# Top-32 attention and a mixture of experts on one core: the query tile's fill one step earlier, a full slot chosen in nine operations, logits laid out in the order of their sum

## The chip, the core and the metric

The kernel runs on one core of a Trainium2 chip. A core has TensorE (PE, matrix products; PEld is its weight load), VectorE (DVE), ScalarE (ACT), GpSimd (POOL) and SyncE (SP), which issues most transfers. GpSimd can issue transfers too, and here it issues the indirect ones, whose rows go where a list of indices says. The metric is the device time of one execution in microseconds (us); a lower one is better.

## What is computed

The reference, cut to what matters:

```
scores = (q @ k.T) / sqrt(64)                      # batch 8, heads 8, 576 x 576
kth    = 32nd largest of each row
attn   = exp(scores - max) where scores >= kth, else 0;  divided by its sum
x      = (attn @ v), heads side by side            # 4608 tokens x 512
logits = x @ w_gate + modality_bias[modality_id]   # 8 experts
e      = argmax(logits);  gate = softmax(logits)[e]
out    = gate * (relu(x @ w1[e]) @ w2[e])          # 512 -> 1024 -> 512
```

## The kernel before

**Attention.** The 64 heads are taken in 32 pairs. A pair has nine tiles of 128 query rows: four for each head and one (role 8) that holds the last 64 rows of both. The main loop runs over steps `i`, one tile each; `p, j = divmod(i, 9)` are the pair and its step. A tile passes through the engines over several steps: TensorE makes the scores two steps ahead (`qk`), ScalarE copies them to `Ssb` (`sevac`), VectorE finds candidates with eight-way maxima (`subs`, `chain`: L375 to L388), ScalarE counts by a sign (`sign`, L407, tile `K`), GpSimd multiplies scores and signs (`pool_y`, L413, tile `y`), VectorE takes the maximum over `y` (`find`, L417) and so the 32nd value (`pick`, L424 to L426), ScalarE takes exponentials and VectorE masks and sums them (`keep`, L437); TensorE transposes and multiplies with V. `KB=2` tiles `K` and `YB=3` tiles `y` exist, so a late `y` holds up the sign two tiles on.

**GpSimd's order in a step** is the order of the code: `gate` (L460, one element, it waits for VectorE's mask of the tile before), `pool_y`, at most one indirect transfer (`posted`, `sends` or `puts`, each followed by a memset of `spare`, L516), `below` (L400, a scalar for the sign), every third step `small` (L394), and in step 5 of a pair `fill`. An engine runs its queue in order, so what stands behind a waiting instruction waits too.

**The query tile.** The role 8 tile of the next pair needs its two halves of queries as a block-diagonal matrix `qbd`. `fill` (L325) copies them from `st` in two instructions of 64 partitions each; TensorE uses the result in step 7 (`qk` of the tile two steps on, L363). In the program the second of the two waits for the completion of the indirect transfers that GpSimd issued since the fill before.

**Tokens and experts.** After each batch (four pairs) the rows are normalized, the logits formed (`logit_rows`, L544 to L564), the expert chosen (`route`), and the rows sent to lists by expert in memory: five indirect transfers, one a step (L590, `xs`). When a list holds enough rows, a slot of 256 is chosen (`sched`), its rows and weights are loaded, and TensorE works on it in the gaps (`expert`, L755 to L787), with a budget that grows by a fixed amount a step and by 0.1 for each small operation of VectorE; the 128 result rows of each half go out by an indirect transfer (L792, `puts`). `whole` says that a slot is sure to be full. The remaining slots are worked on behind the attention (from about 1030 us), with `slot` and `choose`.

**What else the change touches.** `base` and `roff` (128x8) hold where each expert's list ends and how far it has been taken; `ie` and `rev` are iotas over the experts; `dot(x, y)` multiplies with the one-hot `oh` and leaves the sum in an accumulator. `lt` holds the logits' parts (two heads `h` of four pairs `a`), over which one VectorE instruction sums.

Of the kernel before, what the change touches and what calls it, by code (L numbers as in the profile page):

```python
# [9 lines left out]
FT = mybir.dt.float32  # L10
# [62 lines left out]
def kernel(  # L73
# [120 lines left out]
    base = const.tile([128, E], FT, name="base")  # L194
    roff = const.tile([128, E], FT, name="roff")
    tokb = const.tile([128, 5], FT, name="tokb")
# [213 lines left out]
    def pool_y(i):  # L410
        t = T[i]
        t["y"] = wk.tile([128, S], FT, name="y", bufs=YB)
        G.tensor_tensor(t["y"], t["S"], t["K"], op=OP.mult)  # L413
# [134 lines left out]
    def logit_rows(u, L, lg):  # L548

        for c0, n, r in ((0, 4, 128), (4, 1, 64)):  # L550
            ps = psX.tile([128, n, HP, 32], FT, name="X")
            for c in range(n):
                PE.transpose(ps[:r, c].rearrange("p a e -> p (a e)"), L[:, (c0 + c) * 128:(c0 + c) * 128 + r], idf)
            lt = const.tile([128, n, HP, 2, E], FT, name=f"lt{n}", bufs=1)
            if n == 1:
                late.append(lambda ps=ps, lt=lt, r=r, c0=c0: V.tensor_tensor(
                    lt[:r, 0], ps[:r, 0, :, :2 * E].rearrange("p a (h e) -> p a h e", h=2),
                    RD[u][:r, :, 2 * c0:2 * c0 + 2][:, :, :, None].to_broadcast([r, HP, 2, E]), op=OP.mult))
            for h in range(2 if n > 1 else 0):
                d = RD[u][:r, :, 2 * c0 + h:2 * (c0 + n):2].rearrange("p a c -> p c a")  # L560
                late.append(lambda h=h, d=d, ps=ps, lt=lt, r=r, n=n: V.tensor_tensor(
                    lt[:r, :, :, h, :], ps[:r, :, :, h * E:h * E + E],
                    d[:, :, :, None].to_broadcast([r, n, HP, E]), op=OP.mult))
            late.append(lambda lt=lt, r=r, c0=c0, n=n: V.tensor_reduce(  # L564
                lg[:r, c0:c0 + n, :], lt[:r].rearrange("p c a h e -> p c e (a h)"), axis=AX.X, op=OP.add))

# [69 lines left out]
    def sched(s, whole):  # L636
# [17 lines left out]
            lambda: V.max(m8, key),  # L654
            lambda: V.tensor_scalar(oh, key, m8[:, 0:1], None, op0=OP.is_equal),
            lambda: dot(n_, av_),
        ]
        if whole:
            pick += [lambda: V.tensor_scalar(full, n_, float(SLOT), None, op0=OP.is_ge),
                     lambda: dot(at, roff, full)]  # L660
        else:
            pick += [lambda: V.scalar_tensor_tensor(a8, base, -float(SLOT), eoff, op0=OP.add, op1=OP.max),
                     lambda: V.tensor_tensor(a8, a8, roff, op=OP.min),
# [4 lines left out]
                     lambda: V.tensor_scalar(mk, pos, at, r1, op0=OP.add, op1=OP.is_lt),  # L668
                     lambda: V.tensor_tensor(mk, mk, ft, op=OP.mult)]
        pick += [lambda: dot(sc[:, 0:1], ie),  # L670
                 lambda: V.tensor_scalar(ei, sc[0:1, 0:2], float(ZROW), None, op0=OP.add)]
        done = [
            lambda: V.tensor_scalar(n_, full if whole else n_, float(SLOT), None, op0=OP.mult if whole else OP.min),
            lambda: V.scalar_tensor_tensor(roff, oh, n_, roff, op0=OP.mult, op1=OP.add),
# [375 lines left out]
    for i in range(LAST):  # L1050
# [175 lines left out]
        if ok(i - LY):  # L1226
            pool_y(i - LY)
        for x in puts:
            x[0] -= 1
# [8 lines left out]
        if ok(i - 2) and (i - 2) % 3 == 2:  # L1238
            small(i - 4)
        if j == 5 and p + 1 < NPAIR:  # L1240
            fill(p + 1, qbd[(p + 1) % 2])
        if i == CLOSE:
# [161 lines left out]
```

## Time and profile before

| | |
|---|---|
| median of three runs | 1251.16 us (1250.37 to 1253.58) |
| the profiled execution | 1252.88 us, of it 1251.1 the span from the first to the last instruction |
| busy, share of the span | PE 94%, PEld 73%, DVE 91%, ACT 79%, POOL 54% |
| granted TensorE clock, mean | 0.982 |
| indirect transfers of GpSimd in the program's run | 40 of `xs`, 26 of L792, 12 of L1020 |

An engine's busy share is a mean over stages with different limits: which one limits is read from stretches and from what each engine waited for. A VectorE or GpSimd row's duration includes what it lost to another engine while it ran.

### The profile page before, as it was taken

The numbers are of one execution on the slowest core, as the hardware profiler recorded it, in microseconds if no ns is written. First come the engines' busy times: TensorE is split into PE (matmuls) and PEld (weight loads), VectorE is DVE, ScalarE is ACT, GpSimd is POOL, SyncE is SP. The second block draws the span as 40 slices with busy tenths as digits, with TensorE's granted clock in tenths as the row PEclk, the third lists the DMA queues.
The fourth block names the chain that finished last, engine by engine and source line by source line (L and its number), as shares of the span: only waits on it lengthen the run. The fifth ranks groups of instructions, "written<-read, shape, count | busy, mean of one in ns | idle before, by whom it ended". The sixth has DMA issues, their size and how long they took to land.

```text
span 1251.1 us, 28550 instructions
## 1 busy us (share of the span) xinstructions
PE 1170.1 (94%) x7962; PEld 915.7 (73%) x7962; DVE 1135.7 (91%) x5890; ACT 987.9 (79%) x2014; POOL 670.7 (54%) x1253
## 2 busy tenths in 40 slices
PE   8888887899997999999999999999999999999995
PEld 6666665767866868777777777786868775689895
DVE  6999998999999999999999999999999995477761
ACT  4899986888888889888889888888889885355542
POOL 5888866555575557554665566555765573210110
PEclk6999998999999999999999999999999999999998
DMA  4663336676347646666566666666576434477650
GB/s 98 166 173 94 85 85 174 165 188 166 89 110 198 184 127 171 178 163 153 157 173 182 169 175 184 177 177 160 153 202 174 122 102 143 156 259 257 217 181 14
DMA packets 204327, 197.13 MB, mean 158 GB/s; under 512 B 104413, under 2 KB 151533, under 8 KB 204160
## 3 DMA queue, kind: packets, MB, share of 16 engines
q1 hardware_dynamic: 196880, 175.92, 52.4%
q0 software_dynamic: 6080, 19.00, 4.1%
q8 instruction: 66, 1.08, 0.4%
q14 instruction: 101, 0.83, 0.2%
q10 hardware_dynamic: 1200, 0.30, 0.1%
HBM read 118.63 MB, written 24.23 MB: 114 GB/s over the span
## 4 chain that ended last, share of the span: by engine, by line
DVE 63%; PE 27%; issue 3%; DMA 2%; POOL 2%; ACT 2%; SPq 0%; POOLq 0%; DVEq 0%
DVE cand L375 17%; DVE mg L417 12%; DVE P L437 11%; PE E L777 4%; PE X L1014 4%; DVE cand L386 4%; PE X L998 3%; PE E L765 3%; DVE cand L387 3%; PE X L499 2%; DVE mg L388 2%; DVE mg L386 2%; DVE mg L387 2%; PE S L363 2%; PE T L471 2%
## 5 line engine op out<-in xcount | busy, mean ns | idle before, releaser
L375 DVE MAX8 cand<-Ssb 128x8 f32<-128x82 f32 (+1 forms) x2016 | 434.6, 234 | 5.6 <-ACT Ssb L368 5.6
L413 POOL TENSOR_TENSOR y<-Ssb,K 128x576 f32<-128x576 f32 x288 | 367.7, 1277 | 4.4 <-ACT K L407 4.0
L407 ACT ACTIVATE K<-Ssb,n 128x576 bf16<-128x576 f32 x288 | 228.1, 792 | 35.8 <-POOL y L413 34.4
L363 PE MATMUL S<-ks,qs 128*128 128x288 f32 x992 | 220.6, 344 | 22.4 <-ACT Ssb L368 19.3
L368 ACT ACTIVATE Ssb<-S 128x576 f32<-128x576 f32 x284 | 186.1, 655 | 66.0 <-PE S L363 31.3
L417 DVE MAX8 mg<-y 128x8 f32<-128x576 f32 x288 | 215.3, 748 | 6.8 <-POOL y L413 6.8
L765 PE MATMUL E<-xgT,w1b 128*128 128x256 f32 x816 | 196.9, 384 | 10.9 <-ACT hT L769 9.2
L363 PEld LDWEIGHTS S<-ks,qs 128*128 128x128 f32 x992 | 150.9, 189 | 70.8 <-ACT Ssb L368 34.7
L431 ACT ACTIVATE ex<-Ssb,sm 128x576 f32<-128x576 f32 x256 | 200.8, 784 | 0.0
L479 ACT ACTIVATE PT<-T 128x640 f32<-128x640 f32 (+1 forms) x288 | 191.2, 664 | 5.8 <-PE T L471 5.8
L437 DVE SCALAR_TENSOR_TENSOR P<-Ssb,kth,ex 128x576 f32<-128x576 f32 x230 | 192.9, 839 | 1.5 <-ACT ex L431 1.2
L777 PE MATMUL E<-w2b,hT 128*128 128x512 f32 x400 | 187.4, 597 | 2.1 <-ACT hT L769 2.0
L471 PE MATMUL T<-idf,P 128*128 128x128 f32 x1152 | 169.7, 274 | 6.3 <-ACT P L456 6.3
L765 PEld LDWEIGHTS E<-xgT,w1b 128*128 128x128 f32 x816 | 148.4, 190 | 36.0 <-ACT hT L769 13.3
L471 PEld LDWEIGHTS T<-idf,P 128*128 128x128 f32 x1152 | 137.4, 141 | 14.9 <-ACT P L456 10.7
L499 PE MATMUL X<-PT,vm 128*64 128x256 f32 (+1 forms) x1536 | 146.6, 333 | 1.8 <-DVE x L533 1.2
L460 POOL TENSOR_SCALAR spare<-P 1x1 f32<-1x1 f32 x230 | 42.0, 182 | 194.7 <-DVE mg L386 177.4
L400 POOL TENSOR_SCALAR n<-mg 128x1 f32<-128x1 f32 x288 | 75.2, 261 | 98.6 <-DVE mg L388 88.7
L499 PEld LDWEIGHTS X<-PT,vm 128*64 128x64 f32 x1536 | 88.3, 138 | 47.3 <-issue 10.7
L777 PEld LDWEIGHTS E<-w2b,hT 128*128 128x128 f32 x400 | 70.6, 190 | 62.9 <-issue 57.7
L1020 POOL DMA_INDIRECT out_dram<-ot,tk x12 | 12.0, 998 | 99.6 <-ACT ot L1019 99.6
L386 DVE MAX8 mg<-cand 128x8 f32<-128x56 f32 x288 | 61.9, 215 | 0.2
(232 smaller groups left out, 2221.6 us busy)
## 6 DMA issues: line engine op xcount, KB each, us to landing
w1b<-in_moe_w_dram SPq DMA_DIRECT2D x76, 512.0 KB
w2b<-in_moe_w_dram SPq DMA_DIRECT2D x76, 512.0 KB
ks<-st SPq DMA_DIRECT2D x62, 288.0 KB
ks<-st SPq DMA_DIRECT2D x62, 256.0 KB
qs<-st SPq DMA_DIRECT2D x124, 128.0 KB
xg<-xs SPq DMA_DIRECT2D x19, 516.0 KB
km<-in_k_dram SPq DMA_DIRECT2D x64, 128.0 KB
vm<-in_v_dram SPq DMA_DIRECT2D x32, 256.0 KB
```

The costliest lines, as they stand in the source:

```text
L363: PE.matmul(ps[:, hf, :288], l, m, start=(n == 0), stop=(n == len(terms) - 1))
L375: return [lambda s=s: V.max(c[:, s * 8:s * 8 + 8], T[i]["S"][:, bnd[s]:bnd[s + 1]]) for s in range(NSUB)]
L407: A.activation(t["K"], t["S"], AF.Sign, scale=2.0 ** -24 - 1.0, bias=t["n"][:, 1, i % 3:i % 3 + 1], accum_out=t["n"][:, 0, i % 3:i % 3 + 1])
L413: G.tensor_tensor(t["y"], t["S"], t["K"], op=OP.mult)
L417: V.max(t["mg"][:, i % 3, 24:32], t["y"])
L431: A.activation(t["ex"], t["S"], AF.Exp, bias=t["s"][:, i % 3:i % 3 + 1])
L437: V.scalar_tensor_tensor(t["P"], t["S"], kth[:, i:i + 1], t["ex"], op0=OP.is_ge, op1=OP.mult, accum_out=dn)
L471: PE.transpose(T[i]["pt"][:, x, :], (Pm if c == 4 else Pb[c % 2])[:, h * 512 + x * 128:h * 512 + x * 128 + 128], idf)
L479: A.activation(o, T[i]["pt"][:, :n], AF.Copy)
L499: PE.matmul(o.rearrange("p (a b) -> p a b", a=2) if j < 8 else o, l, r, start=(c == 0), stop=(c == 4))
L765: PE.matmul(ps[:, f % 2], w1b[:, c, f * 128:(f + 1) * 128], xgT[:, c, :], start=(c == 0), stop=(c == KC - 1))
L777: PE.matmul(o["py"], hT[:, f, t * 128:(t + 1) * 128], w2b[:, f, :], start=(f == 0), stop=(f == FC - 1))
```

## The change

Three edits. `fill` is issued in step 4 of a pair, right behind `pool_y` and ahead of the step's transfer, instead of in step 5 at the end. For a full slot, `oh` is one-hot times "the list holds at least 256", a product with `er` (the expert's number and its `roff` side by side) and one sum give both numbers that SyncE loads, and `roff` grows by 256 where `oh` is 1: nine operations of VectorE instead of eleven, none with an accumulator. `lt` is laid out so that the sum reads it in order, and the products ahead of it write it with a step.

```
     base = const.tile([128, E], FT, name="base")
-    roff = const.tile([128, E], FT, name="roff")
+    er = const.tile([128, 2, E], FT, name="er")
+    G.iota(er[:, 0, :], pattern=[[1, E]], base=0, channel_multiplier=0, allow_small_or_imprecise_dtypes=True)
+    roff = er[:, 1, :]
+    zc = const.tile([1, 2], FT, name="zc")
+    G.memset(zc[:, 0:1], 0.0)
+    G.memset(zc[:, 1:2], float(ZROW))
...
-            lt = const.tile([128, n, HP, 2, E], FT, name=f"lt{n}", bufs=1)
+            lt = const.tile([128, n, E, HP, 2], FT, name=f"lt{n}", bufs=1)
...
-                    lt[:r, :, :, h, :], ps[:r, :, :, h * E:h * E + E],
+                    lt[:r, :, :, :, h].rearrange("p c e a -> p c a e"), ps[:r, :, :, h * E:h * E + E],
                     d[:, :, :, None].to_broadcast([r, n, HP, E]), op=OP.mult))
             late.append(lambda lt=lt, r=r, c0=c0, n=n: V.tensor_reduce(
-                lg[:r, c0:c0 + n, :], lt[:r].rearrange("p c a h e -> p c e (a h)"), axis=AX.X, op=OP.add))
+                lg[:r, c0:c0 + n, :], lt[:r].rearrange("p c e a h -> p c e (a h)"), axis=AX.X, op=OP.add))
...
             lambda: V.max(m8, key),
-            lambda: V.tensor_scalar(oh, key, m8[:, 0:1], None, op0=OP.is_equal),
-            lambda: dot(n_, av_),
         ]
         if whole:
-            pick += [lambda: V.tensor_scalar(full, n_, float(SLOT), None, op0=OP.is_ge),
-                     lambda: dot(at, roff, full)]
+            both = const.tile([128, 2, E], FT, name="s_er")
+            ea = const.tile([128, 2], FT, name="s_ea")
+            pick += [lambda: V.tensor_scalar(full, m8[:, 0:1], float(SLOT * E), None, op0=OP.is_gt),
+                     lambda: V.tensor_scalar(oh, key, m8[:, 0:1], full, op0=OP.is_equal, op1=OP.mult),
+                     lambda: V.tensor_tensor(both, er, oh[:, None, :].to_broadcast([128, 2, E]), op=OP.mult),
+                     lambda: V.tensor_reduce(ea, both, axis=AX.X, op=OP.add),
+                     lambda: V.tensor_tensor(ei, ea[0:1, :], zc, op=OP.add)]
...
-        pick += [lambda: dot(sc[:, 0:1], ie),
-                 lambda: V.tensor_scalar(ei, sc[0:1, 0:2], float(ZROW), None, op0=OP.add)]
-        done = [
-            lambda: V.tensor_scalar(n_, full if whole else n_, float(SLOT), None, op0=OP.mult if whole else OP.min),
+        done = [lambda: V.scalar_tensor_tensor(roff, oh, float(SLOT), roff, op0=OP.mult, op1=OP.add)] if whole else [
+            lambda: V.tensor_scalar(n_, n_, float(SLOT), None, op0=OP.min),
             lambda: V.scalar_tensor_tensor(roff, oh, n_, roff, op0=OP.mult, op1=OP.add),
         ]
...
         if ok(i - LY):
             pool_y(i - LY)
+        if j == 4 and p + 1 < NPAIR:
+            fill(p + 1, qbd[(p + 1) % 2])
...
         if ok(i - 2) and (i - 2) % 3 == 2:
             small(i - 4)
-        if j == 5 and p + 1 < NPAIR:
-            fill(p + 1, qbd[(p + 1) % 2])
```

A slot that may be part full keeps its operations. The order on the engines shows where rows have moved. On GpSimd, in a pair with an output transfer in step 5 (the fill at about 862 us before), the rows before were these (`y` is the product, `n` below's scalar, `spare` gate's element or the memset, `qbd` the fill's two instructions):

```order
L413 TENSOR_TENSOR y<-Ssb,K 128x576
L792 DMA out_dram<-ot,stok_130 4608x512
L516 MEMSET spare 1x1
L400 TENSOR_SCALAR n<-mg 128x1
L325 TENSOR_SCALAR qbd_116<-st 64x2x64 x2
L460 TENSOR_SCALAR spare<-P_120 1x1
L413 TENSOR_TENSOR y<-Ssb,K 128x576
L400 TENSOR_SCALAR n<-mg 128x1
```

and in the change these, from the step before on:

```order
L418 TENSOR_TENSOR y<-Ssb,K 128x576
L330 TENSOR_SCALAR qbd_116<-st 64x2x64 x2
L405 TENSOR_SCALAR n<-mg 128x1
L399 TENSOR_SCALAR sm<-mg 128x3
L701 TENSOR_SCALAR sgt_138<-xg 128x2
L702 TENSOR_SCALAR stok_131<-xg 128x2
L465 TENSOR_SCALAR spare<-P_119 1x1
L418 TENSOR_TENSOR y<-Ssb,K 128x576
L405 TENSOR_SCALAR n<-mg 128x1
L465 TENSOR_SCALAR spare<-P_120 1x1
L418 TENSOR_TENSOR y<-Ssb,K 128x576
L802 DMA out_dram<-ot,stok_130 4608x512
```

The fill stood two rows behind the transfer; now it stands two products ahead of it, because here the transfer has moved a step later as well. In a batch, on GpSimd again (the fill at about 767 us before), the fifth row transfer and the output transfer came first:

```order
L590 DMA xs<-x_152,dest 38912x516
L516 MEMSET spare 1x1
L400 TENSOR_SCALAR n<-mg 128x1
L394 TENSOR_SCALAR sm<-mg 128x3
L460 TENSOR_SCALAR spare<-P_119 1x1
L413 TENSOR_TENSOR y<-Ssb,K 128x576
L792 DMA out_dram<-ot,stok_130 4608x512
L516 MEMSET spare 1x1
L400 TENSOR_SCALAR n<-mg 128x1
L325 TENSOR_SCALAR qbd_115<-st 64x2x64 x2
```

and in the change the fill comes ahead of both:

```order
L418 TENSOR_TENSOR y<-Ssb,K 128x576
L330 TENSOR_SCALAR qbd_115<-st 64x2x64 x2
L595 DMA xs<-x_156,dest 38912x516
L521 MEMSET spare 1x1
L405 TENSOR_SCALAR n<-mg 128x1
L399 TENSOR_SCALAR sm<-mg 128x3
L465 TENSOR_SCALAR spare<-P_119 1x1
L418 TENSOR_TENSOR y<-Ssb,K 128x576
L802 DMA out_dram<-ot,stok_130 4608x512
```

Of the batch's five row transfers four are still ahead of the fill, the last of them one step. On VectorE, where a full slot is chosen (the slot at 677 us before), the rows before were

```order
L652 TENSOR_TENSOR s_av<-base,roff 128x8
L653 SCALAR_TENSOR_TENSOR s_key<-s_av,rev 128x8
L654 MAX s_m_11586<-s_key 128x8
L655 TENSOR_SCALAR s_oh<-s_key,s_m_11586 128x8
L650 SCALAR_TENSOR_TENSOR s_jk,s_sc<-s_oh,s_av 128x8
L659 TENSOR_SCALAR s_sc<-s_sc 128x1
L650 SCALAR_TENSOR_TENSOR s_jk,s_sc<-s_oh,s_sc,roff 128x8
L650 SCALAR_TENSOR_TENSOR s_jk,s_sc<-s_oh,ie 128x8
L671 TENSOR_SCALAR sei_133<-s_sc 1x2
```

and in the change

```order
L657 TENSOR_TENSOR s_av<-base,er 128x8
L658 SCALAR_TENSOR_TENSOR s_key<-s_av,rev 128x8
L659 MAX s_m_11590<-s_key 128x8
L664 TENSOR_SCALAR s_sc<-s_m_11590 128x1
L665 TENSOR_SCALAR s_oh<-s_key,s_m_11590,s_sc 128x8
L666 TENSOR_TENSOR s_er<-er,s_oh 128x16
L667 TENSOR_REDUCE s_ea<-s_er 128x2
L380 MAX cand<-Ssb 128x8
L668 TENSOR_TENSOR sei_133<-s_ea,zc 1x2
```

The three rows with an accumulator (`s_jk,s_sc`) are gone, a product and a sum over `s_er` have come, and a maximum of the attention (`cand`) now stands between.

## Rows read from the trace of the kernel before

**Rows 1.** Windows: busy us (instructions) by engine, granted clock, DMA share, GB/s.
```profile
200.00:600.00 400.00, 372.79 (x2587) 288.05 (x2586) 392.31 (x2189) 346.95 (x714) 226.13 (x435) 0.99 0.62 161
600.00:1030.00 430.00, 422.64 (x2814) 326.21 (x2813) 425.95 (x2314) 373.56 (x770) 259.50 (x510) 1.00 0.61 166
1030.00:1251.00 221.00, 204.60 (x1241) 168.16 (x1239) 128.77 (x354) 101.93 (x165) 35.96 (x80) 0.98 0.52 174
```
In each row the engines stand as PE, PEld, DVE, ACT, POOL.

**Rows 2.** The page's chain that ended last, share of the span by engine.
```profile
DVE 63%; PE 27%; issue 3%; DMA 2%; POOL 2%; ACT 2%; SPq 0%; POOLq 0%; DVEq 0%
```

**Rows 3.** The fill's line L325: GpSimd idle before it until (us, times).
```profile
  DMA out_dram<-ot,stok: 14.5, 6
  issue: 8.5, 3
  DMA xs<-x,dest: 5.0, 1
  DVE ks L272: 4.0, 1
  POOL qbd L325: 0.4, 1
```

**Rows 4.** GpSimd's timeline about 862 us: start, duration, instruction [idle before].
```profile
859.99 1.06 POOL L792 DMA_INDIRECT out_dram<-ot,stok  x1 [0.17 <-ACT K L407]
...
864.14 0.30 POOL L325 TENSOR_SCALAR qbd<-st 64x128 fp32r<-64x128 f32 x1 [2.03 <-DMA out_dram<-ot,stok]
...
864.67 1.27 POOL L413 TENSOR_TENSOR y<-Ssb,K 128x576 f32<-128x576 f32 x1
```

**Rows 5.** GpSimd's timeline about 210 us.
```profile
205.81 0.96 POOL L590 DMA_INDIRECT xs<-x,dest  x1 [0.17 <-issue]
...
212.87 0.30 POOL L325 TENSOR_SCALAR qbd<-st 64x128 fp32r<-64x128 f32 x1 [5.04 <-DMA xs<-x,dest]
```

**Rows 6.** VectorE's timeline about 215 us.
```profile
214.71 0.76 DVE L417 MAX8 mg<-y 128x8 f32<-128x576 f32 x1 [3.12 <-POOL y L413]
...
215.65 0.84 DVE L424 TENSOR_TENSOR eq<-i9s,n 128x27 f32<-128x27 f32 x1
```

**Rows 7.** VectorE's waits from 30 to 1010 us: in total, times, longest.
```profile
DVE mg L417 <- POOL y L413: 6.8, 5, 3.1
```

**Rows 8.** The line L613, a product of route: duration in ns, min/median/max.
```profile
L613 DVE TENSOR_TENSOR r_pr<-r_pb,ohb x8: 180/413/1350, 185.6 to 1075.9; 128x40 f32<-128x40 f32 x8
```

**Rows 9.** VectorE's timeline about 995 us, the last of the ten.
```profile
995.27 1.13 DVE L612 TENSOR_TENSOR r_pb<-r_rk,base 128x40 f32<-128x40 f32 x1
```

**Rows 10.** GpSimd's timeline in a batch, about 363 us.
```profile
362.32 1.03 POOL L590 DMA_INDIRECT xs<-x,dest  x1 [0.17 <-issue]
...
363.99 1.28 POOL L413 TENSOR_TENSOR y<-Ssb,K 128x576 f32<-128x576 f32 x1
```

**Rows 11.** VectorE's timeline where the slot at 677 us is chosen.
```profile
678.07 0.17 DVE L650 SCALAR_TENSOR_TENSOR s_jk<-s_oh,s_av 128x8 f32<-128x8 f32 x1
...
678.28 0.15 DVE L659 TENSOR_SCALAR s_sc<-s_sc 128x1 f32<-128x1 f32 x1
678.47 0.23 DVE L650 SCALAR_TENSOR_TENSOR s_jk<-s_oh,s_sc,roff 128x8 f32<-128x8 f32 x1
...
678.95 0.16 DVE L671 TENSOR_SCALAR sei<-s_sc 1x2 int32<-1x2 f32 x1
```

**Rows 12.** VectorE's groups by line and shape: busy us, mean ns.
```profile
L1001 DVE SCALAR_TENSOR_TENSOR hl<-X,hh 128x256 fp32r<-128x256 f32 x36 | 15.2, 423 | 21.3 <-ACT hh L1000 21.3
L564 DVE TENSOR_REDUCE lgb<-lt 128x32 f32<-128x256 f32 x8 | 4.8, 606 | 0.0
L655 DVE TENSOR_SCALAR s_oh<-s_key,s_m 128x8 f32<-128x8 f32 x19 | 4.3, 224 | 0.3
L668 DVE TENSOR_SCALAR smk<-pos,s_sc 128x2 f32<-128x2 f32 x11 | 3.0, 274 | 0.0
```

**Rows 13.** TensorE's timeline about 770 us.
```profile
770.77 1.56 PE L765 MATMUL E<-xgT,w1b 128*128 128x256 f32 x6 [1.40 <-ACT hT L769]
```

More of the change, by code (lines that the diff above doesn't have):

```diff
@@ L553, in logit_rows @@
                 PE.transpose(ps[:r, c].rearrange("p a e -> p (a e)"), L[:, (c0 + c) * 128:(c0 + c) * 128 + r], idf)
-            lt = const.tile([128, n, HP, 2, E], FT, name=f"lt{n}", bufs=1)
+            lt = const.tile([128, n, E, HP, 2], FT, name=f"lt{n}", bufs=1)
             if n == 1:
                 late.append(lambda ps=ps, lt=lt, r=r, c0=c0: V.tensor_tensor(
-                    lt[:r, 0], ps[:r, 0, :, :2 * E].rearrange("p a (h e) -> p a h e", h=2),
+                    lt[:r, 0].rearrange("p e a h -> p a h e"), ps[:r, 0, :, :2 * E].rearrange("p a (h e) -> p a h e", h=2),
                     RD[u][:r, :, 2 * c0:2 * c0 + 2][:, :, :, None].to_broadcast([r, HP, 2, E]), op=OP.mult))
@@ L654, in sched @@
             lambda: V.max(m8, key),
-            lambda: V.tensor_scalar(oh, key, m8[:, 0:1], None, op0=OP.is_equal),
-            lambda: dot(n_, av_),
         ]
         if whole:
-            pick += [lambda: V.tensor_scalar(full, n_, float(SLOT), None, op0=OP.is_ge),
-                     lambda: dot(at, roff, full)]
-        else:
-            pick += [lambda: V.scalar_tensor_tensor(a8, base, -float(SLOT), eoff, op0=OP.add, op1=OP.max),
+            both = const.tile([128, 2, E], FT, name="s_er")
[5 more added lines that the diff above has]
+                     lambda: V.tensor_tensor(ei, ea[0:1, :], zc, op=OP.add)]
+        else:
+            pick += [lambda: V.tensor_scalar(oh, key, m8[:, 0:1], None, op0=OP.is_equal),
+                     lambda: dot(n_, av_),
+                     lambda: V.scalar_tensor_tensor(a8, base, -float(SLOT), eoff, op0=OP.add, op1=OP.max),
                      lambda: V.tensor_tensor(a8, a8, roff, op=OP.min),
@@ L668, in sched @@
                      lambda: V.tensor_scalar(mk, pos, at, r1, op0=OP.add, op1=OP.is_lt),
-                     lambda: V.tensor_tensor(mk, mk, ft, op=OP.mult)]
-        pick += [lambda: dot(sc[:, 0:1], ie),
-                 lambda: V.tensor_scalar(ei, sc[0:1, 0:2], float(ZROW), None, op0=OP.add)]
-        done = [
-            lambda: V.tensor_scalar(n_, full if whole else n_, float(SLOT), None, op0=OP.mult if whole else OP.min),
+                     lambda: V.tensor_tensor(mk, mk, ft, op=OP.mult),
+                     lambda: dot(sc[:, 0:1], ie),
+                     lambda: V.tensor_scalar(ei, sc[0:1, 0:2], float(ZROW), None, op0=OP.add)]
+        done = [lambda: V.scalar_tensor_tensor(roff, oh, float(SLOT), roff, op0=OP.mult, op1=OP.add)] if whole else [
+            lambda: V.tensor_scalar(n_, n_, float(SLOT), None, op0=OP.min),
             lambda: V.scalar_tensor_tensor(roff, oh, n_, roff, op0=OP.mult, op1=OP.add),
```

## The prediction

> **What bounds the kernel now.** I read the stretches first. From 200 to 600 us VectorE is busy for 392.31 of 400 us, from 600 to 1030 for 425.95 of 430 [rows 1]. TensorE is busy for 372.79 of 400 in the first and for 422.64 of 430 in the second, so it has 27.2 us of room in the first and 7.4 in the second; behind 1030 VectorE falls to 128.77 of 221 and TensorE is the busy one. The chain of work that ended last gives VectorE 63% and TensorE 27% [rows 2]. So time is won where VectorE stands still or is slowed between 200 and 1030 us, and past 600 TensorE soon stands next in line.
>
> Then I read who holds GpSimd up at the query tile's fill (`fill`, L325). The tile's two instructions run back to back in most pairs, but in ten pairs the second waits: 14.5 us in six of them for an output row's transfer, 5.0 us once for a row transfer, 8.5 us in three that the view puts down to issue [rows 3]; an eleventh waits 0.4 us on GpSimd. All eleven fills stand behind an indirect transfer that GpSimd itself issued a moment ago. One output transfer is issued at 859.99; the fill's second half starts only at 864.14, 2.03 us of it spent waiting, 4.15 us after that issue [rows 4]. Behind it stands the product `y` (L413), which starts at 864.67, late.
>
> What a late `y` costs VectorE has two forms. The maximum over `y` (L417) waits for it: 3.12 us at 214.71, behind the longest fill wait, 5.04 us at 212.87 [rows 5, 6]; five such waits, 6.8 us in all [rows 7]. And VectorE operations with two inputs are stretched while `y` runs: L613 takes 180 ns at best and 1350 at worst [rows 8], the worst at 864.65, beside the `y` of 864.67. I find ten such operations within 12 us behind a waiting fill, from L424 at 215.65 (0.84 instead of 0.17 us) to L612 at 995.27 (1.13 instead of 0.19) [rows 6, 9]; over the median of their kind they lose 8.3 us together. So the eleven waits cost VectorE 6.8 + 8.3 = 15.1 us. Place by place: five fills stand behind an output transfer alone (one in 200 to 600, four later); they cost 6.3 us, 1.9 of it in the first stretch and 4.4 in the second. Six stand behind a batch of row transfers; they cost 8.8 us: 3.8, 1.5 and 0 before 600, and 0.7, 1.3 and 1.4 after. Fill waits of 1.6 to 2.0 us cost 0.7 to 1.2 us each, waits of 3.0 to 3.6 us cost 1.3 to 1.5.
>
> **The fill's move.** The fill is now issued one step earlier and ahead of that step's transfer. Behind an output transfer alone nothing is left to wait for: the order of GpSimd shows no transfer in the two steps ahead of these five fills. So 6.3 us go, 1.9 before 600 and 4.4 after. TensorE uses the tile three steps later, so being early costs it nothing.
>
> In the six batches the fill now stands one step behind a row transfer, where it stood behind a later one. In the step at 362.32 a transfer is issued, and the next `y` ends at 363.99 + 1.28 = 365.27 [rows 10]; the fill's second half, 0.3 us after the first, would come at 365.6, 3.3 us after the issue. From issue to the second half took 4.15 us at 859.99 and 7.06 us at 205.81 [rows 4, 5], the ten waiting places 3.7 to 7.1. So 0.4 to 3.8 us of wait stay in each batch, also at the place where now it is 0.4. I take 2 us. Queued behind it on GpSimd are this step's row transfer, `below`'s scalar, `gate` and the next `y`; as now, VectorE waits for that `y`. A price of 1.2 us per batch, between 1.0 (the mean of the 1.6 to 2.0 us waits) and 1.4, gives 7.2 us in place of 8.8. Before 600 that saves 5.3 - 3.6 = 1.7 us, after it 3.4 - 3.6 = -0.2. Bounds: nothing left (8.8 saved), or the 3.8 us of the longest wait at all six (22.7 - 8.8 = 13.9 lost).
>
> **The choice of a full slot.** Six slots are chosen in the new way between 600 and 1030, two more later, where VectorE has room. Removed are three dot products with accumulator; in the slot at 678, where they stand back to back, the first takes 0.21 us from its start to the next start (678.07 to 678.28), the other two 0.48 (678.47 to 678.95) [rows 11]; the one scalar in `done` is small and I count it at 0.05. Added are a product and a sum over 16 elements, for which I take 0.19 us each, as from 678.28 to 678.47 between dependent neighbours. The one-hot now has two scalars from memory: 274 against 224 ns [rows 12], 0.05. Together 0.74 - 0.43 = 0.3 us; interleaved with maxima an added one costs nearer 0.11, and 0.5 us are saved. I take 0.4, times six: 2.4 us. Bounds: 0 (the new ones as dear as the old) to 3. The fewer small operations also lower the budget for TensorE's expert work, and six output products move one step later; their number stays, and I count that at nothing, since TensorE works without a break there.
>
> **The logits' layout.** The sum over 256 elements reads with a step of eight words and takes 606 ns; an operation that passes through 256 elements takes 423 [rows 12]. In order it may save 0.18 us in each of eight batches, 1.5 in all. The two products ahead of it now write with that step, 256 elements together. If a write with a step costs what the read cost, the whole saving is gone; I take that, 0, with 1.5 us saved as the other bound. The Trainium skill speaks against this part: "Vector Engine (DVE) Microarchitecture Reference", section "5.2 Measured stream behaviour on trn2 (trn3 not measured)", measures 2.50 ns an element for a destination that steps by 24 words, against 1.05 in order, and by that estimate the writes would lose 0.37 us a batch where the sum wins 0.18, 1.5 us slower over eight. No row here has such a write.
>
> The three constants at the start are one more iota and two one-element fills on GpSimd, where it idles 4.0 us ahead of the first fill [rows 3]: nothing; without that cover under 1 us.
>
> **The sum.** Before 600: 1.9 + 1.7 = 3.6 us, and TensorE's 27.2 us of room take it. After 600: 4.4 - 0.2 + 2.4 = 6.6 us for VectorE, against TensorE's 7.4 us of idle time. Part of that idle time comes from the same late `y`: at 770.77 TensorE waited 1.40 us for ScalarE's hT [rows 13], which stood behind a sign that waited for `y`. That part goes with the waits, the rest does not. I take two thirds, 4.4 us (bounds 0 and 6.6). Together 8.0 us: the profiled execution, 1252.9 us (a span of 1251.1 and 1.8 around it), would come to 1244.9. The median of the runs lies 1.7 us below it, so the forecast is 1251.2 - 8.0 = 1243.2 us.
>
> **The rivals.** (a) The row transfers land in time and the batches cost nothing: 3.6 + 3.6 = 7.2 us before 600, and after it 6.6 + 3.6 = 10.2, cut to TensorE's 7.4: 14.6 us, 1236.6. For it speaks the 0.4 us wait; against it that transfers took at least 3.7 us and the fill comes at 3.3. (b) TensorE takes over past 600: only the 3.6 us come, 1247.6. For it speaks TensorE's 422.64 of 430; against it the chain's 63% on VectorE. (c) Slower: in the batches the waiting fill now holds back a row transfer that used to go ahead of it, GpSimd has no pause to catch up there, and each batch costs what the worst costs now, 3.8 us: 13.9 lost, 6.3 + 2.4 won, 1256.4. It decides the sign from (8.8 + 6.3 + 2.4) / 6 = 2.9 us a batch on; the 3.0 to 3.6 us waits cost 1.3 to 1.5, which speaks against it. (d) The new choice is no shorter: then 1.6 us less are won, 1244.8, inside the first case.
>
> **How the numbers follow.** Chances: the forecast's case 0.64, own range 1240 to 1247; (a) 0.10; (b) 0.20; (c) 0.06. A measurement of this kernel can tell about 0.3%, 3.75 us: faster is below 1247.4, slower above 1254.9. Faster: 0.64 + 0.10 and a tenth of (b), 0.75; slower 0.06; same 0.19. The range from 1237 to 1249 leaves out (c), about half of (a) and the edge of (b).
>
> **What would show it.** In the profile after, the fill's idle time should fall from 28.0 us to about 12, all of it behind row transfers; L417's waits from 6.8 us to under 3; L613's worst to under 0.5 us unless a batch is near. VectorE's busy time should fall by about 6 us, part in the stretches. The three dot products' lines should be gone for full slots, with a product and a sum of about 0.2 us each. L564's mean should fall towards 0.42 us while the two products ahead of it (L561) become dearer by about as much. I am wrong if the fill's waits stay above 20 us, if TensorE's busy time past 600 fills its stretch without the stretch becoming shorter, or if the batches' stretched rows grow.

## The result and the profile after

The changed kernel took 1239.69 us (median of five runs, 1238.38 to 1242.16) beside 1251.95 for the kernel before (five runs): a ratio of 0.990, 95% interval 0.9887 to 0.9913, about 12 us. The profiled execution took 1242.16 us with a span of 1240.4, 10.7 less than before. The forecast was 1243.2, its range 1237 to 1249. One execution of a kernel further down (the choice with the old list length) took 1666.55 us at a granted clock of 0.651 and is left out of its ratio.

In the changed kernel the lines stand five further down from `fill` (L330) to the logits, ten further down from the end of `sched` on: `y` is L418, the maximum over it L422, the mask L442, the logits' products L561 and L566 and their sum L569, the row transfers L595, the output transfers L802.

The windows of the changed kernel, columns as in [rows 1]:

```profile
200.00:600.00 400.00, 378.23 (x2600) 293.08 (x2599) 396.18 (x2209) 346.60 (x716) 223.73 (x443) 0.99 0.63 162
600.00:1030.00 430.00, 424.44 (x2835) 328.25 (x2835) 425.06 (x2296) 376.34 (x776) 256.80 (x512) 1.00 0.61 168
1030.00:1251.00 221.00, 195.63 (x1196) 162.28 (x1192) 117.83 (x300) 94.62 (x151) 29.37 (x69) 0.98 0.49 164
```

VectorE does more in the first stretch (396.18 us against 392.31) because less of it is idle; from 600 on it and TensorE are both almost full, and both were. What was won shows in the last stretch, which now ends 10.7 us earlier: VectorE has 117.83 us left there, where it had 128.77.

The chain that ended last, by engine, answers to [rows 2]. VectorE's part fell, TensorE's rose from 27%:

```profile
DVE 50%; PE 37%; ACT 4%; issue 3%; DMA 3%; POOL 2%; SPq 0%; POOLq 0%; ACTq 0%; DVEq 0%
```

The fill's line, with what its idle time waited for, answers to [rows 3]; the fence behind it has VectorE's wait from 30 to 1030 us, which answers to [rows 7]:

```profile
L330 POOL TENSOR_SCALAR qbd<-st x62: 287/294/804, 23.1 to 977.4; 64x128 fp32r<-64x128 f32 x62
...
  DMA xs<-x,dest: 10.1, 5
  DVE ks L277: 3.8, 1
  issue: 3.3, 1
```
```profile
DVE mg L422 <- POOL y L418: 3.0, 4, 1.0
```

No wait for an output transfer is left (14.5 us in six places before). 10.1 + 3.3 = 13.4 us remain, all in the six batches, where I expected about 12. VectorE's wait for `y`, 3.0 us, is at the bound that I expected. L618, the product of [rows 8], takes 604 ns at worst instead of 1350, and VectorE's busy time fell by 9.0 us (1126.7) where I expected 6. Where an output transfer stood ahead of the fill, as at 859.99 in [rows 4], GpSimd's timeline now reads

```profile
847.49 0.66 POOL L330 TENSOR_SCALAR qbd<-st 64x128 fp32r<-64x128 f32 x2
...
853.83 1.27 POOL L418 TENSOR_TENSOR y<-Ssb,K 128x576 f32<-128x576 f32 x1
855.27 1.05 POOL L802 DMA_INDIRECT out_dram<-ot,stok  x1 [0.17 <-ACT ex L436]
```

The fill's two instructions run back to back, and the transfer comes two products behind them. In a batch the wait has stayed. GpSimd's and VectorE's timelines about 880 us:

```profile
876.68 1.02 POOL L595 DMA_INDIRECT xs<-x,dest  x1 [0.17 <-issue]
...
883.24 0.29 POOL L330 TENSOR_SCALAR qbd<-st 64x128 fp32r<-64x128 f32 x1 [3.35 <-issue]
883.91 0.98 POOL L595 DMA_INDIRECT xs<-x,dest  x1 [0.38 <-POOL qbd L330]
...
885.66 1.28 POOL L418 TENSOR_TENSOR y<-Ssb,K 128x576 f32<-128x576 f32 x1
...
888.72 1.27 POOL L418 TENSOR_TENSOR y<-Ssb,K 128x576 f32<-128x576 f32 x1
```
```profile
886.97 0.76 DVE L422 MAX8 mg<-y 128x8 f32<-128x576 f32 x1 [1.03 <-POOL y L418]
...
888.73 1.29 DVE L665 TENSOR_SCALAR s_oh<-s_key,s_m,s_sc 128x8 f32<-128x8 f32 x1
```

The second half of the fill follows the row transfer of 876.68 by 6.56 us, the next row transfer and `y` are late, VectorE waits 1.03 us for that `y`, and the new one-hot (L665, 0.29 us alone) takes 1.29 us beside the next one. It does so in all three batches past 600 (1.29 to 1.31 us; 0.27 to 0.29 in the other five slots).

How long the second half waits goes with the load on the DMA engines. In the 3.2 us behind the last row transfer ahead of the fill their share is 0.50 in the second batch (from 356.31 us), where the wait is 0.42 us, and 0.92 to 1.0 in the other five, where it is 1.37 to 3.35 us. That the load is the cause is not shown: the fill's move alone, below, has one batch with 0.55 and 2.00 us.

**A measure by tile.** All kernels here run the maximum over `y` 288 times in the same order, so the start of the k-th in the kernel before, less the start of the k-th in another kernel, is the time by which the other is ahead there. The first part, up to the tile at 51 us, moved by -1.5 to +3.2 us. Most of this stands at the first maximum already (-0.6 to +3.2 us) and I take it for scatter of single executions, since the fill's move alone has +3.24 and with the other edits -1.40; an effect of the edits of about 1 us isn't ruled out there. The table gives this part apart. In us, with the runs that follow, times as in the trace of the kernel before:

| kernel | to 51 | 51 to 168 | 168 to 598 | 598 to 1047 | ratio to before, 95% interval |
|---|---|---|---|---|---|
| changed | -1.40 | 3.24 | 3.99 | 5.12 | 0.990 (0.9887 to 0.9913) |
| changed, again | -1.08 | 3.24 | 4.34 | 5.46 | 0.9907 (0.9893 to 0.9922) |
| fill moved alone | 3.24 | 2.96 | 1.55 | 1.66 | 0.9949 (0.9932 to 0.9965) |
| choice alone | 0.94 | 0.06 | 1.18 | 5.53 | 0.9947 (0.9934 to 0.9960) |
| logits alone | 0.86 | 0.32 | 1.26 | 1.40 | 0.9984 (0.9973 to 0.9995) |
| choice, old list length | 0.13 | 0.03 | 1.50 | 2.09 | 0.9983 (0.9974 to 0.9993) |
| old choice, new list length | 0.41 | -0.07 | 1.23 | 1.86 | 0.9995 (0.9986 to 1.0005) |
| old place, no wait | -0.10 | 0.02 | 5.21 | 6.43 | 0.9912 (0.9898 to 0.9927) |
| new place, no wait | -1.22 | 2.15 | 5.08 | 6.75 | 0.9908 (0.9886 to 0.9931) |
| changed, old list length | -1.47 | 3.26 | 5.70 | 4.17 | 0.9916 (0.9897 to 0.9935) |
| changed, masked fill | -0.27 | 1.95 | 2.95 | 10.02 | 0.9871 (0.9854 to 0.9887) |
| changed, column fill | -1.43 | 2.33 | 6.13 | 9.78 | 0.9867 (0.9852 to 0.9882) |
| changed, column fill, again | -1.25 | 2.41 | 6.25 | 9.88 | 0.9855 (0.9838 to 0.9871) |

Some 1.3 to 1.6 us of the third column come in the batch near 210 us even in kernels that leave the fill alone: the wait of 5.04 us in [rows 5] was a long one, by chance of that execution (3.43 us in the choice alone, 2.94 in the choice with the old list length).

### The profile page after: what moved, and what is told of

Read it like the earlier page. It is cut to its first block, busy times and chain, and to the rows that moved or that the text cites. A ratio compares the mean times of both kernels' runs of the same rounds, so it can differ in the third digit from the quotient of the medians.

```text
span 1240.4 us, 28518 instructions
## 1 busy us (share of the span) xinstructions
PE 1171.4 (94%) x7962; PEld 919.8 (74%) x7962; DVE 1126.7 (91%) x5850; ACT 985.8 (79%) x2014; POOL 660.1 (53%) x1256
## 3 DMA queue, kind: packets, MB, share of 16 engines
q8 instruction: 66, 1.08, 0.4%
## 4 chain that ended last, share of the span: by engine, by line
DVE 50%; PE 37%; ACT 4%; issue 3%; DMA 3%; POOL 2%; SPq 0%; POOLq 0%; ACTq 0%; DVEq 0%
DVE cand L380 14%; DVE mg L422 9%; DVE P L442 8%; PE E L787 7%; PE E L775 5%; PE X L1024 4%; PE X L504 4%; PE X L1008 4%; PE S L368 3%; DVE cand L391 3%; PE T L476 3%; DVE cand L392 3%; DVE mg L391 2%; DVE mg L393 2%; DVE mg L392 2%
## 5 line engine op out<-in xcount | busy, mean ns | idle before, releaser
L418 POOL TENSOR_TENSOR y<-Ssb,K 128x576 f32<-128x576 f32 x288 | 367.4, 1276 | 5.7 <-ACT K L412 5.1
L422 DVE MAX8 mg<-y 128x8 f32<-128x576 f32 x288 | 214.5, 745 | 3.3 <-POOL y L418 3.3
L775 PE MATMUL E<-xgT,w1b 128*128 128x256 f32 x816 | 199.8, 388 | 5.7 <-ACT hT L779 4.2
L442 DVE SCALAR_TENSOR_TENSOR P<-Ssb,kth,ex 128x576 f32<-128x576 f32 x230 | 188.5, 820 | 1.7 <-ACT ex L436 1.5
L405 POOL TENSOR_SCALAR n<-mg 128x1 f32<-128x1 f32 x288 | 72.5, 252 | 97.5 <-DVE mg L393 87.8
L914 PE MATMUL E<-onesb 128*128 128x256 bf16 x412 | 60.6, 287 | 1.8 <-DVE onesb L150 1.2
```

The lines of the kernel that those rows point to most:

```text
L422: V.max(t["mg"][:, i % 3, 24:32], t["y"])
L442: V.scalar_tensor_tensor(t["P"], t["S"], kth[:, i:i + 1], t["ex"], op0=OP.is_ge, op1=OP.mult, accum_out=dn)
L775: PE.matmul(ps[:, f % 2], w1b[:, c, f * 128:(f + 1) * 128], xgT[:, c, :], start=(c == 0), stop=(c == KC - 1))
```

## The experiments

My theory after the result: the fill's place and its wait carry most of the 12 us, the choice and the logits 1 to 2 us each. The rival: choice and logits carry a third or more.

**The fill's move alone** (the kernel before with this only):

```
             pool_y(i - LY)
+        if j == 4 and p + 1 < NPAIR:
+            fill(p + 1, qbd[(p + 1) % 2])
...
-        if j == 5 and p + 1 < NPAIR:
-            fill(p + 1, qbd[(p + 1) % 2])
```

> Before, with nothing but the fill's move. Theory (the fill's place and wait carry most): 8 to 11 us faster than before, 1241 to 1244 us; the fill's idle time about 13 us, all in the six batches; L437 in pairs 1 to 4 at 0.95 us everywhere, where before has one of 1.7 us in each; no stretched row in the slots' choice, since the one-hot with two scalars is not there. Rival (the slot's choice and the logits carry a third or more of the 12 us): 5 to 7 us faster only, 1245 to 1247.

Measured: 1245.24 us against 1252.83 (median of the runs beside it), ratio 0.9949: by the ratio 6.4 us of 12.5 (the medians lie 7.6 us apart; one of the six executions took 1250.16 us). The mechanism is as expected (12.0 + 3.2 us of waits left, all in batches), the size is that of the rival.

**The choice alone.**

```
+            pick += [lambda: V.tensor_scalar(full, m8[:, 0:1], float(SLOT * E), None, op0=OP.is_gt),
+                     lambda: V.tensor_scalar(oh, key, m8[:, 0:1], full, op0=OP.is_equal, op1=OP.mult),
...
+        done = [lambda: V.scalar_tensor_tensor(roff, oh, float(SLOT), roff, op0=OP.mult, op1=OP.add)] if whole else [
```

> Before, with nothing but the new choice of a full slot. Theory: 0.3 to 0.4 us less in each slot, some of it given back where the one-hot with two scalars lies beside a late y: 1 to 2 us faster, 1250 to 1251. Rival (the choice carries a third): 4 us faster, 1248. Second rival (the stretched one-hot eats it all): no change within 0.5 us.

Measured: 1245.85 us, ratio 0.9947, 6.6 us: as much as the fill's move, and far over my 1 to 2. The columns of the table say where: nothing early, 5.53 us past 598. There the three places near 750, 880 and 1010 us gain 1.18, 1.20 and 0.98 us, and exactly these places gain 1.15, 1.17 and 0.93 us with the fill's move alone. The fill's waits in the choice alone, and GpSimd's timeline near 860 us, where [rows 4] had the transfer first:

```profile
POOL qbd L330 <- DMA out_dram<-ot,stok: 8.6, 3, 4.0
```
```profile
855.74 0.67 POOL L330 TENSOR_SCALAR qbd<-st 64x128 fp32r<-64x128 f32 x2
...
858.82 1.06 POOL L802 DMA_INDIRECT out_dram<-ot,stok  x1 [0.17 <-ACT ex L436]
```

The fill waits for an output transfer three times instead of six, and its idle time there is 5.9 us less: the shorter list gives TensorE's expert work a smaller budget, three output products come a step later, and their transfers now stand behind the fill instead of ahead of it. Two edits took away the same three waits, which is why the parts (6.4 + 6.6 + 2.0 = 15.0 us by their ratios) add up to more than the whole (12.5): three places, 3.4 us by the choice alone, are counted twice. The tiles past 598 show the same excess: 1.66 + 5.53 + 1.40 = 8.59 us against 5.12.

**The logits alone.**

```
-                    lt[:r, :, :, h, :], ps[:r, :, :, h * E:h * E + E],
+                    lt[:r, :, :, :, h].rearrange("p c e a -> p c a e"), ps[:r, :, :, h * E:h * E + E],
...
-                lg[:r, c0:c0 + n, :], lt[:r].rearrange("p c a h e -> p c e (a h)"), axis=AX.X, op=OP.add))
+                lg[:r, c0:c0 + n, :], lt[:r].rearrange("p c e a h -> p c e (a h)"), axis=AX.X, op=OP.add))
```

> Before, with nothing but the logits' new layout. Theory (from the trace after: a batch gains about 0.2 us, though the sum and the two products trade their time): 1 to 1.6 us faster. The prediction's own value: no change. The rule that writes with a step cost more than reads with one: 1.5 us slower. The two products' rows should be at 385 ns, the sum's at 405, as after.

Measured: 1250.89 us, ratio 0.9984, 2.0 us (0.6 to 3.4). VectorE's groups in the changed kernel show that the durations cancel, 606 ns to 405 for the sum, 280 to 385 for each of two products; [rows 12] has the sum before:

```profile
L566 DVE TENSOR_TENSOR lt<-X,rd 128x128 f32<-128x128 f32 x16 | 6.0, 385 | 0.8 <-PE X L558 0.8
...
L569 DVE TENSOR_REDUCE lgb<-lt 128x32 f32<-128x256 f32 x8 | 3.2, 405 | 0.0
```

The time comes from what a duration doesn't say. VectorE's timeline of one batch, before and in the changed kernel, a product and a sum each with the row that starts next:

```profile
448.53 0.28 DVE L561 TENSOR_TENSOR lt<-X,rd 128x128 f32<-128x128 f32 x1
448.73 0.75 DVE L417 MAX8 mg<-y 128x8 f32<-128x576 f32 x1
...
450.33 0.60 DVE L564 TENSOR_REDUCE lgb<-lt 128x32 f32<-128x256 f32 x1
450.85 0.24 DVE L375 MAX8 cand<-Ssb 128x8 f32<-128x82 f32 x1
```
```profile
441.67 0.39 DVE L566 TENSOR_TENSOR lt<-X,rd 128x128 f32<-128x128 f32 x1
441.88 0.74 DVE L422 MAX8 mg<-y 128x8 f32<-128x576 f32 x1
...
443.47 0.41 DVE L569 TENSOR_REDUCE lgb<-lt 128x32 f32<-128x256 f32 x1
443.79 0.24 DVE L380 MAX8 cand<-Ssb 128x8 f32<-128x82 f32 x1
```

From the product's start to the next start it is 0.20 us before and 0.21 now, although its duration grew by 0.11: the longer write lies beside the next instruction. From the sum's start to the next it is 0.52 us before and 0.32 now. So a batch gains 0.2 us, as the tiles' lead shows at the logits of the seven batches up to 1030 us (0.22 to 0.28 each, 1.7 in all). In these seven other instructions stand between the second product and the sum that reads it. In the eighth, behind the loop, nothing does, and there the longer write counts: from the first product's start to the sum's it is 0.52 us before (1064.64 to 1065.16) and 0.66 now (1053.97 to 1054.63). The Trainium skill's "Perfetto Trace Analysis", section "Optimizing Scalar/DVE Operations", says of the access overhead that its profiled latency is about twice the engine's busy time, since the half that acknowledges the write overlaps with the next instruction. These rows agree in that a row lasts longer than it holds the engine (0.28 us against 0.20); the factor isn't tested here. The Trainium skill's rule that I had weighed against this part ("Vector Engine (DVE) Microarchitecture Reference", section "5.2 Measured stream behaviour on trn2 (trn3 not measured)") is for a step of 24 words. As an estimate for these short writes with a step of eight words it was too high: in the seven batches they hold up the next instruction by 0.01 to 0.04 us each, not by 0.18.

**The old place without the wait**, to tell place and wait apart. One instruction over all 128 partitions, which in the program waits for no transfer:

```
     def fill(p, bd):
-        for h in range(2):
...
+        q = PR[p]["st"][:, :, 1, 512:].bitcast(FT)
+        G.tensor_tensor(bd.rearrange("p x (h s) -> p x h s", h=2), q[:, :, None, :].to_broadcast([128, 2, 2, 64]),
+                        fm[:, None, :, :].to_broadcast([128, 2, 2, 64]), op=OP.mult)
```

`fm` (128x2x64) is 1 where the partition belongs to the half and 0 elsewhere.

> Before, with the fill in its old place, ahead of y in the sixth step, but as one instruction over all 128 partitions with a mask of zeros and ones as second input, which waits for no transfer. Theory (what costs is mainly the wait, 15.1 us of it by the trace before; the place alone costs 0.7 us in each of the four early pairs): 9 to 12 us faster, 1240 to 1243, with the fill's idle time near 4 us, all at the first fill, and L437 still at 1.7 us once in pairs 1 to 4. Rival (the place costs, since 0.6 us of GpSimd ahead of y are late in every pair): 3 to 5 us faster at most.

Measured: 1241.97 us, ratio 0.9912, 11.0 us, with no wait at the fill but the first. Taking away the wait alone, in the old place, is worth more than moving the fill. But it gains nothing in the four early pairs (0.02 us in the table), where the fill's move gains 2.96. There no indirect transfer is issued yet, and what counts is the place. GpSimd's and VectorE's timelines before, about 55 us, then the changed kernel's:

```profile
53.83 0.67 POOL L325 TENSOR_SCALAR qbd<-st 64x128 fp32r<-64x128 f32 x2
54.58 1.28 POOL L450 TENSOR_TENSOR ex<-Ssb,hT 128x576 f32<-128x576 f32 x1
55.82 1.28 POOL L413 TENSOR_TENSOR y<-Ssb,K 128x576 f32<-128x576 f32 x1
```
```profile
56.03 1.68 DVE L437 SCALAR_TENSOR_TENSOR P<-Ssb,kth,ex 128x576 f32<-128x576 f32 x1
```
```profile
55.23 1.29 POOL L455 TENSOR_TENSOR ex<-Ssb,hT 128x576 f32<-128x576 f32 x1
56.48 1.29 POOL L418 TENSOR_TENSOR y<-Ssb,K 128x576 f32<-128x576 f32 x1
```
```profile
57.43 0.94 DVE L442 SCALAR_TENSOR_TENSOR P<-Ssb,kth,ex 128x576 f32<-128x576 f32 x1
```

In the old place the fill's 0.67 us put `ex` and `y` later; VectorE's mask then starts 0.21 us behind `y`'s start instead of 0.95 and takes 1.68 us instead of 0.94. The same row, with 1.62 us at 56.13, is in the run without the wait. The Trainium skill's "SBUF — State Buffer", section "Who interferes with whom", says that a VectorE instruction with two inputs from memory contends with a GpSimd instruction that reads it; these rows agree.

**The choice with the old list length, and the old choice with the new one.** Two empty entries keep the list at eleven (the second stands behind the update of `roff`); in the second kernel two pairs of the old operations are handed out as one entry each (the second pair are the two of that update):

```
+                     lambda: None,
                      lambda: V.tensor_tensor(ei, ea[0:1, :], zc, op=OP.add)]
```
```
+            one, two_ = pick[-4:-2], pick[-2:]
+            pick[-4:] = [lambda: [f() for f in one], *two_]
```

> Before with the new choice of a full slot, and two empty entries in its list, so that the list is as long as the old one and the three output products stay in their old steps, ahead of the fill. Theory (the choice alone was worth 7 us because its shorter list moves three output transfers from just ahead of the fill to a step behind it; the operations themselves save only 0.45 us in each of three slots and little elsewhere): 1.5 to 3 us faster than before, 1250 to 1251.5, and the fill again waits six times for an output transfer. Rival (the operations save it themselves): as the choice alone, 1245 to 1247.

> Before with all the old operations of the choice, but two pairs of them handed out as one entry each, so that the list is as short as the new one and the three output products move a step. Theory: the three places near 750, 880 and 1010 us gain 1.0 to 1.2 us each, 3 to 4 us faster than before, 1248.5 to 1250, with three waits for an output transfer left. Rival (the step of the products is worth nothing, as the prediction had it): no change.

Measured: 1250.07 us, ratio 0.9983, 2.1 us for the operations alone, as the theory had it. The list's length alone gives 1251.69 us, ratio 0.9995: not told from no change, where I expected 3 to 4 us. Its waits for output transfers are the three that were expected, and its tiles gain 1.20, 1.21 and 0.98 us at the three places, but 0.52 and 0.40 us are lost in two batches and 0.1 us in many places, so that 1.86 us of lead remain past 598; and the profiled execution, 1249.23 us, was the fastest of its eleven. The waits in the two runs:

```profile
POOL qbd L330 <- DMA out_dram<-ot,stok: 13.6, 6, 4.0
```
```profile
POOL qbd L325 <- DMA out_dram<-ot,stok: 9.1, 3, 4.0
```

2.1 + 0.6 us are less than the 6.6 of the choice alone. By tiles, past 598, it is 2.09 + 1.86 against 5.53. So the two work together, and I can't split the rest: handing out two dependent operations in one step is itself a change.

**The changed kernel with the old list length**, by the same two empty entries.

> After, with two empty entries in the full slot's list, so that the three output products stand in their old steps again, right behind the fill of the step before. Theory (the fill's move and the shorter list take away the same three waits, so that with the fill moved the list's length is worth nothing): the same as after within 1 us, 1239 to 1241, no wait for an output transfer at the fill. Rival (the later step of the products is worth its 1.2 us three times whatever the fill does): 1242.5 to 1244.

Measured: 1242.71 us, ratio 0.9916. The time lies in the rival's range and not in mine, but the interval overlaps with the changed kernel's, so the two aren't told apart. No wait for an output transfer is left, and the three places gain 1.16, 1.17 and 0.94 us as in the changed kernel (1.26, 1.26, 1.04), so the rival's reason falls: with the fill moved, the later transfer is worth nothing there. But 1.25 and 1.98 us are lost at two places, near 850 and 980 us. VectorE's timeline there, and TensorE's:

```profile
959.38 0.40 DVE L566 TENSOR_TENSOR lt<-X,rd 128x128 f32<-128x128 f32 x1 [1.24 <-PE X L558]
...
975.28 0.69 DVE L538 TENSOR_TENSOR x<-X,rd 128x512 f32<-128x512 f32 x1 [0.78 <-PE X L537]
```
```profile
957.23 0.59 PE L776 MATMUL E<-xgT,w1b 128*128 128x256 f32 x2
...
958.74 0.71 PE L558 MATMUL X<-idf,x 128*128 128x128 f32 x5
```

VectorE waits for the transposes behind the expert products (L776): with the longer list TensorE is given more expert work than it has time for. It is rival (b) of the prediction, in two spots. In the changed kernel the first of the two waits has 0.5 us in all and the second 0.6.

It also wins where I expected nothing: in the last two batches the fill's second half waits 0.42 us and not at all (3.20 and 3.35 in the changed kernel), the share of the DMA engines behind the row transfer is 0.50 in both (0.92), and the two batches are 1.3 and 2.1 us better than the changed kernel's. So by tiles it isn't behind: the last one is 11.66 us ahead, where the changed kernel's two executions have 10.95 and 11.96.

**The changed kernel with a fill that waits for nothing**, masked as above, or as two products with a column of zeros and ones:

```
+            G.tensor_scalar(bd[:, :, r], PR[p]["st"][:, :, 1, 512:].bitcast(FT), fm[:, h:h + 1], None, op0=OP.mult)
```

> After, with the fill in its new place as one masked instruction over 128 partitions that waits for no transfer. Theory (after still loses to the waits of the six batches, and the place alone is worth 3 us in the early pairs): 3 us come before 600 us and 4.6 after, which TensorE's 5.6 us of room there may take: 5 to 7 us faster than after, 1233 to 1235, and no wait at the fill but the first. Rival (TensorE takes over past 600): 3 us, about 1237. Second rival (the masked product takes 0.94 us instead of 0.67 and gives it back): no better than after.

> After, with the fill as two instructions over all 128 partitions, each times a column of zeros and ones; neither waits for a transfer. Theory: as the masked product or up to 2 us faster, since the two take about 0.67 us and not 0.94: 1231 to 1234. Rival (TensorE takes over past 600): about 1237, as the masked product. Second rival (the longer product costs nothing): the same time as the masked product within 0.5 us.

Measured: 1237.18 and 1236.44 us, ratios 0.9871 and 0.9867. Both lie over my ranges, where the rivals put them (about 1237), and the two aren't told apart. The masked product takes 0.73 us here; the 0.94 of the expectation was a mean over the old place, where 11 of 31 took 1.24 to 1.39 us beside VectorE's mask. **And place and wait together** (the fill's move and the masked product), without the other edits:

> Before, with the fill moved and as one masked instruction that waits for no transfer (old choice, old logits). It completes the four cases of place and wait. Theory: against the masked fill in its old place (1242.0 us) the new place gives 0.45 us in each of the four early pairs, 1.9, and nothing elsewhere: 1239.5 to 1241; against the moved fill that still waits (1245.2) the six batches' waits go, 4 to 6 us. Rival (the place is worth as much again later on): 1237 or less. Second rival (without the wait the place is worth nothing): 1242.

Measured: 1240.64 us, ratio 0.9908, as my theory had it. By tiles the place adds the 2.13 us of the early pairs to the old place without the wait; the ratios don't tell the two apart. Against the moved fill that still waits, 4.6 us are won. **Last, the changed kernel and its column version on one chip:**

> The changed kernel itself, unaltered, on the same chip as the column version. Theory: 12 us faster than before, 1239.5 to 1241.

> The column version again (the changed kernel, its fill as two instructions over all 128 partitions that wait for no transfer), beside the changed kernel on the same chip. Theory (the six batches still cost the changed kernel 3 to 5 us): 3 to 4 us faster than the changed kernel, 1236 to 1237.5. Rival (the 3 us between them were the difference of two chips): within 1 us of the changed kernel.

Measured: 1241.07 (1239.79 to 1241.85) and 1234.64 us (1233.60 to 1235.87): 6.4 us between them, with no overlap, more than the 3 to 4 that I expected (5.3 by the last tile). The ratio to before is 0.9855 for the column version, the fastest kernel here. Its window past 600, its fill's group and its only wait at the fill:

```profile
600.00:1030.00 430.00, 427.74 (x2872) 331.08 (x2871) 427.01 (x2300) 378.06 (x780) 268.35 (x515) 1.00 0.61 168
```
```profile
L335 POOL TENSOR_SCALAR qbd<-st,fm 128x128 fp32r<-128x128 f32 x62 | 37.1, 601 | 0.0
```
```profile
POOL qbd L335 <- DVE ks L277: 3.7, 1, 3.7
```

The fill takes 1.2 us now, nearly twice what I expected of it, and it still wins: in the six batches its tiles' lead changes by +3.06, +1.51, -0.15, +0.65, +1.26 and +1.34 us, where the changed kernel has +2.73, +0.91, -1.47, -0.77, -0.61 and -0.68. TensorE is busy for 427.74 of 430 us and VectorE for 427.01.

## Why the prediction was right, and where its terms were off

**Output transfers: right.** 6.3 us were to go in full, 1.9 and 4.4. The tiles gain 1.40 us at the one place before 600, and 1.11, 1.26, 1.26 and 1.04 at the four later: 1.40 + 4.67 = 6.1.

**The batches: the mechanism right, the price low.** I took 2 us of wait in each and 1.2 us of cost; the wait is 13.4 / 6 = 2.2 us. The six changes of lead just given sum to +0.11 us where 1.7 - 0.2 = 1.5 was forecast: with 8.8 us spent before, (8.8 - 0.1) / 6 = 1.45 us each. Measured from the column version, whose fill doesn't wait and whose six changes sum to 7.7, it is (7.7 - 0.1) / 6 = 1.3. Of the first batch's 2.73 us 1.3 to 1.6 are the chance named above, so against an ordinary execution the batches lost 1.2 to 1.5 us. Past 600 the late `y` meets the new one-hot (1.29 to 1.31 us) in each; the fill's move alone, with the old operations, pays about as much there (-0.87, -1.03 and -0.68 us), so the edit of the choice is not the reason. As rival (c) had it, the waiting fill holds up the row transfer behind it; what that alone costs was not measured, and the price stayed under the 2.9 us that would turn the sign.

**The early pairs: missed.** 0.74 us in each of four pairs, 3.0 in all, were no term. I had looked for the fill's cost where it waits, and costed its 0.67 us of work at nothing; the mask of 1.68 us at 56.03 was to be read in the trace before.

**The choice: the operations about right, the order missed.** 0.4 us a slot holds where they stand back to back: 0.46, 0.47 and 0.48 us of lead at three slots; at the three woven ones it is 0.05 to 0.29 in the choice alone. A seventh slot falls into the stretch (at 1027.6 us before) and gains 0.34. The operations alone gave 2.1 us against 2.4. The second scalar of the one-hot, put at 0.05 us, costs 0.06 (0.29 us against 0.23) but 1.0 more where a late `y` runs beside it. But "I count that at nothing" of the six output products that move a step was wrong: three of them carry a transfer past the fill, 3.4 us. In the changed kernel as a whole this is hidden, because the fill's move had taken the same waits away.

**The logits: 0 was too low.** The runs show 2.0 us (0.6 to 3.4), the tiles 1.7 in seven of eight batches, about the bound of 1.5. The failing step is "if a write with a step costs what the read cost, the whole saving is gone": the durations do cancel, but a longer write hardly holds up the next instruction, as long as that one doesn't read what was written.

**The cut by TensorE: wrong for this sum.** I let a third of 6.6 us past 600 be lost; the tiles gain 5.12 us there, the four output places (4.67 against 4.4) and the choice (2.3 against 2.4) in full, and what went was lost in the batches (-2.06 against -0.2). That TensorE becomes the limit beyond the changed kernel is likely, not shown: VectorE waits 0.5 us for the logits' transposes in the changed kernel and 1.7 with the old list length, and in the column version both engines are busy for 427 of 430 us.

**The sum.** Uncut, my terms were 3.6 + 6.6 = 10.2 us. By the tiles of the profiled execution what they name brought 8.5 us: 6.1 at the output places, 2.3 in the choice, 0.1 in the batches. The early pairs (3.0) and seven batches' logits (1.7) came on top, and 1.4 went at the start and 0.8 in small steps elsewhere: 11.0, and the last tile is 10.95 us ahead. So that the forecast lay within 3.5 us of the median is in part luck: 4.7 us that I had missed stood against batches that brought less and a start that came later. The cut, which didn't happen, made the forecast too careful. Rival (a), the batches for nothing, is the column version; its 1236.6 us were close to the 1236.44 and 1234.64 measured, though its sum lacks the early pairs and the logits as well.

**Left open:** why the program lets the form on partitions 64 to 127 wait for the transfers and not the one on all 128, how the list's length and the new operations gain more together than apart, what makes a batch's wait 0 us in one kernel and 3.35 in another, and why the fill's place counts in the early pairs alone.

## What to carry to other kernels

Look at what an instruction costs where it waits for nothing too: 0.67 us of GpSimd in the wrong step cost VectorE 0.74 us in each of four early pairs. When a scheduler counts operations, a shorter list moves other engines' work and transfers past each other, so compare the order and not only the operations; two edits may then take away the same wait. And cost a VectorE instruction from its start to the next start, not by its duration, and mind whether the next one reads its result.

## What the runs showed of the hardware

A VectorE product of 128 elements a partition that writes with a step of eight words takes 385 ns instead of 280, but the next instruction starts only 0.01 to 0.04 us later; the sum that reads the result, right behind two such products, started 0.14 us later. A sum that reads 256 elements with that step holds the next instruction up by 0.20 us. A VectorE one-hot of 8 elements with two scalars from memory took 0.27 to 0.29 us alone and 1.29 to 1.31 beside GpSimd's product `y`. GpSimd took 0.30 us for a 64x128 copy with constant factors, 0.60 for 128x128 with a column as factor, and 0.73 for a 128x256 product in one instruction, which took 1.24 to 1.39 where VectorE's mask of 0.80 us ran beside it; which of partitions and form makes the second twice the first was not tried.
